# A gated attention and state-space kernel on one core: Toeplitz tiles interleaved by channel, convolution results transposed on PE, exps of 3 and 2 banks

## The chip, the cores and the metric

The kernel runs on one core of a Trainium2 chip. Its time is the device time of one execution in microseconds (us). Besides the timed runs there is one profiled execution; all rows below come from it. PE is the matrix engine, PEld its weight loads, ACT the scalar engine (here it computes the exponentials), DVE the vector engine, POOL the general engine and SP the engine that issues most DMAs. PE writes its results to PSUM, which has eight banks of 128 partitions by 512 fp32 numbers; everything else that the engines read lies in SBUF, and DMAs move data between SBUF and DRAM.

## The reference, cut to what matters

```python
x = A_x                                             # 1 x 2048 x 448, bf16
g = sigmoid((x * gate_w).sum(-1, keepdims=True))
q = (x @ wq) in 16 heads of 28;  k = x @ wk;  v = x @ wv     # one key and value head for all
a = softmax(q k^T / sqrt(28)) v, heads joined, @ wo
P = exp(dt * A * l)                                 # 448 x 256 modes, l = 0..2047, complex
K = Re(sum_n C_n P_nl (dt B_n))                     # 448 x 2048: one filter per channel
b = causal_conv(x, K) per channel + x * Dskip
out = g * a + (1 - g) * b
```

The attention has 16 heads over 2048 x 2048 scores. The state-space part (SSM) builds a filter of 2048 taps for each of the 448 channels from 256 complex modes, and convolves each channel of x with its filter.

## The kernel before, in words

**Order of the work.** The program is a list of operations, each with an engine, a cost in ns and keys that it reads and writes. `Prog.schedule` (L104) plays the list through with these costs: of all operations whose inputs are done it takes the one that can start first, and between equals the one with the lower `pr`. The order that comes out is fixed: each engine gets its operations in that order and waits on semaphores of other engines where a key demands it (`emit`, L190). A DMA is planned at 330 bytes per ns and 2 us to land (L55 to L57). A `lock` lets one user after the other hold a PSUM bank. So when an operation is late on the chip, everything behind it on its engine is late too.

**Attention.** The 1024 tiles (4 blocks of 512 queries, 4 groups of 4 heads, 16 key tiles, 4 heads) are cut into 342 batches of 3. `qk` (L842) computes three tiles of scores into banks 0 to 2 or 3 to 5 in turn (L849), ACT takes the exponential of all three in one instruction (L859), and `pv` (L862) multiplies them by the values into bank 6 (`psB`, L874). The three score matmuls of a batch use different 32-row groups of the array, the value matmuls different 32-column groups. After each of 16 groups `norm` (L817) scales by the gate on DVE (L823), sends the denominators through DRAM to spread them (three DMAs in series), and DVE divides (L832) into `onT`. `qproj` (L590) makes the queries two groups ahead, in bank 7 (`psX`).

**SSM.** The channels are cut into 28 chunks of 16. For each, `tables` (L662) raises the modes to powers on DVE by doubling (18 large instructions; `masters` makes the factors for four chunks), and `kgen` (L711) turns them into filters: 64 matmuls (L724) into `psX` in four operations of 16, one DVE copy (L734), four stores to `KP_scratch` in DRAM. `tload` (L741) reads four channels back as a Toeplitz tile: partition p gets the filter from tap p on, which takes a row that starts 2 bytes later for each partition. A tile is 1 MB, loaded by two DMAs of 64 partitions, four runs of 2 KB a partition; four buffers hold tiles (`NTR`). `conv` (L750) multiplies: for each channel 16 blocks of 64 outputs, weights from `U` (x in blocks, 32 columns, zeros where there is no past), moving operand 64 columns of the Toeplitz tile, 64 matmuls a tile (L763), two tiles in one hold of `psX`. DVE copies the result reversed (L770), four stores bring it to `Y_scratch` in DRAM.

`qproj`, `kgen`, `conv` and the projection share `psX` under the lock "X". Chunk `c` of `kgen` and chunk `c - 2` of `conv` are put into the list together, spread evenly between the attention's batches (L893 to L902).

**Output.** After all that the list has, for each of four groups T of 112 channels and each query block qc, `bt` (L778): load y from `Y_scratch` with channels on partitions, add x times Dskip (L786), multiply by 1 - g (L788) into `xT`; and `outg` (L791): for four token tiles four matmuls with Wo (L804) and one with the identity that adds the SSM part (L807), copy (L813), store. T is the outer loop, so the first groups can run once a quarter of the channels is convolved and attention has given `onT`. `osb` has two buffers, `psX` is one bank.

**Start.** `consts` and `loads` zero and load the weights on POOL's queue, x and the raw parameters on SP's and ACT's; `prep_x`, `prep_params` and `prep_attn` transpose x, make the seeds of the modes (`seedz`, `seedw`) and kT, V and the gate. `uload` (L417) loads U for 112 channels by two DMAs with 224-byte runs, four times in the program.

Of the kernel before, what the change touches and what calls it, by code (L numbers as in the profile page):

```python
# [11 lines left out]
P = 128  # L12
# [36 lines left out]
class Op:  # L49
    __slots__ = ("i", "eng", "fn", "ns", "lat", "deps", "pr", "lock", "unlock", "slot", "ndma",  # L50
                 "count", "vc", "end", "nsucc")


class Prog:
    SEM_NS = 60  # L55
    DMA_NS = 2000
    DMA_BW = 330.0  # L57

    def __init__(self, nc, es):
        self.nc, self.es = nc, es  # L60
        self.ops = []
        self.lastw = {}
        self.readers = {}
        self.slots = {}

    def op(self, eng, fn, ns, rd=(), wr=(), pr=0, lat=60, lock=None, unlock=None):
        o = Op()
        o.i, o.eng, o.fn, o.ns, o.lat, o.pr = len(self.ops), eng, fn, ns, lat, pr
        o.lock, o.unlock, o.slot, o.ndma = lock, unlock, None, 0
        deps = {}  # L70
        for k in rd:
            w = self.lastw.get(k)
            if w is not None:
                deps[w] = 1
# [16 lines left out]
    def dma(self, pairs, nbytes, slot, rd=(), wr=(), pr=0, eng="sp", slow=False):  # L91
# [4 lines left out]
        o = self.op(eng, fn, nbytes, rd, wr, pr)  # L96
# [7 lines left out]
    def schedule(self):  # L104
# [15 lines left out]
        locks = {}  # L120
        dmafree = 0.0
        done = 0
        while done < n:
            best = None
            for e in ENG:
                T = free[e]
                for i in ready[e]:
                    o = ops[i]
                    r = max(rt[i], T)
                    if o.lock is not None:  # L130
                        L = locks.setdefault(o.lock, [None, 0.0, []])
                        if L[0] is not None:
                            continue
                        r = max(r, L[1])
                    key = (r, o.pr, i)
                    if best is None or key < best[0]:
                        best = (key, e, i)
            if best is None:
                for L in locks.values():
                    o = ops[L[0]]  # L140
                    print("holder", o.i, o.eng, o.pr, o.fn, [ (j, ops[j].eng, need[j], getattr(ops[j],'end',None)) for j in succ[o.i]])
                    j = [q for q in range(o.i, n) if getattr(ops[q], 'end', None) is None]
                    print([(q, ops[q].eng, ops[q].pr, ops[q].slot, [d for d in ops[q].deps if getattr(ops[d], 'end', None) is None]) for q in j[:30]])
# [9 lines left out]
            order[e].append(i)  # L153
            if o.lock is not None:
# [5 lines left out]
            if o.slot is not None:  # L160
                free[e] = r + 60.0 * o.ndma
                s = max(r, dmafree)
                dmafree = s + o.ns / self.DMA_BW
# [9 lines left out]
            for j in succ[i]:  # L173
# [102 lines left out]
class Kernel:  # L276
# [25 lines left out]
    def alloc(self):  # L302
# [20 lines left out]
        self.rdenB = sb("rdenB", 2 * 512, F32)  # L323
        self.denT = sb("denT", 2 * 16, F32)
        self.onT = sb("onT", 16 * 512, BF)
        self.grow = sb("grow", S, BF)
        self.omg = sb("omg", S, BF)
        self.yT = sb("yT", 2 * 512, BF)
        self.U = sb("U", 2 * 47 * DT, BF)
# [19 lines left out]
        self.osb = sb("osb", 2 * D, BF)  # L349
# [3 lines left out]
        self.Y = nc.dram_tensor("Y_scratch", (D * S,), BF).ap()  # L353
        self.R = nc.dram_tensor("R_scratch", (16 * 4 * 512,), F32).ap()

    def consts(self):
# [16 lines left out]
        pg.op("pool", lambda e: e.memset(V(self.Wq, 0, NT * 512), 0.0), 900, wr=["Wq"])  # L373
        pg.op("pool", lambda e: e.memset(V(self.Wk, 0, NT * P), 0.0), 300, wr=["Wk"])
        pg.op("pool", lambda e: e.memset(self.Wk.v(96, 32, 3 * P + 28, [[32, 4]]), 1.0), 100, wr=["Wk"])
        pg.op("pool", lambda e: e.memset(self.Wk.v(96, 16, 3 * P + 28, [[32, 4]]), 0.0), 100, wr=["Wk"])
        pg.op("pool", lambda e: e.memset(V(self.Wo, 0, NT * D), 0.0), 900, wr=["Wo"])
        pg.op("pool", lambda e: e.memset(V(self.Wb, 0, P), 0.0), 100, wr=["Wb"])
        pg.op("pool", lambda e: e.memset(self.xT.v(96, 32, 3 * S, [[1, S]]), 1.0), 900, wr=["xT3a", "xT3b"])
        pg.op("pool", lambda e: e.memset(self.vaug.v(0, P, 28, [[32, 16]]), 1.0), 100, wr=["va"])  # L380
        pg.op("pool", lambda e: e.memset(self.vaug.v(0, P, 29, [[32, 16], [1, 3]]), 0.0), 100, wr=["va"])
        for s in range(2):
            pg.op("pool", lambda e, s=s: e.memset(self.U.v(0, 64, s * 47 * DT, [[1, 31 * DT]]), 0.0), 2000, wr=[("U", s)], pr=5)
            pg.op("pool", lambda e, s=s: e.memset(self.U.v(64, 64, s * 47 * DT, [[1, 15 * DT]]), 0.0), 2000, wr=[("U", s)], pr=5)
        pg.op("pool", lambda e: e.memset(V(self.kstg, 0, 128), 0.0), 100, wr=[("kst", 0)], pr=5)

    def loads(self):
# [3 lines left out]
        for hf in range(4):  # L391
            pg.dma([(xst.v(0, P, hf * 4 * D, [[D, 4], [1, D]]), dram(x, hf * 4 * P * D, [[D, P], [P * D, 4], [1, D]]))],
                   4 * P * D * 2, f"x{hf}", wr=[("xst", hf)], eng="sp")
        raw = self.onT
        self.names = ["B_A_re", "B_A_im", "B_B_re", "B_B_im", "B_C_re", "B_C_im"]
        pg.dma([(self.dt32.v(0, P, 0, [[1, D]]), dram(ins["B_log_dt"], 0, [[0, P], [1, D]]))], 120000, "ldt", wr=["dt"], eng="act")
        for k, nm in enumerate(self.names):
            pg.dma([(raw.v(0, DT, k * 1024, [[NM, 4], [1, NM]]), dram(ins[nm], 0, [[NM, DT], [DT * NM, 4], [1, NM]]))],
                   D * NM * 2, f"raw{k}", wr=[("raw", k)], eng="act" if k < 2 else "sp", pr=1)
        w = ins["A_wk"]  # L400
        pg.dma([(self.Wk.v(0, DT, 32 * r, [[P, 4], [1, DH]]), dram(w, 0, [[DH, DT], [DT * DH, 4], [1, DH]]))
                for r in range(4)], 400000, "wk", wr=["Wk"], eng="pool")
# [577 lines left out]
```

## Time and profile before

| | us |
|---|---|
| median of 3 runs | 845.64 (844.11 to 847.72) |
| the profiled execution | 844.77 |
| its span, first to last instruction | 843.0 |
| PE busy in the span | 556.3 |
| DVE busy | 525.7 |
| ACT busy | 495.8 |
| POOL busy | 30.1 |

The span is what the profile shows; some 2 us lie around it. Busy times of PE and PEld overlap. The page also has the waits by releaser, the DMA queues and the DMA issues; a time line gives each instruction's start and length from the start of the span.

### The profile page before, as it was taken

The numbers are of one execution on the slowest core, as the hardware profiler recorded it, in microseconds if no ns is written. First come the engines' busy times: TensorE is split into PE (matmuls) and PEld (weight loads), VectorE is DVE, ScalarE is ACT, GpSimd is POOL, SyncE is SP. The second block draws the span as 40 slices with busy tenths as digits, with TensorE's granted clock in tenths as the row PEclk, the third lists the DMA queues.
The fourth block names the chain that finished last, engine by engine and source line by source line (L and its number), as shares of the span: only waits on it lengthen the run. The fifth ranks groups of instructions, "written<-read, shape, count | busy, mean of one in ns | idle before, by whom it ended". The sixth has DMA issues, their size and how long they took to land.

```text
span 843.0 us, 25548 instructions
## 1 busy us (share of the span) xinstructions
PE 556.3 (66%) x11601; PEld 323.5 (38%) x11616; DVE 525.7 (62%) x1153; ACT 495.8 (59%) x362; POOL 30.1 (4%) x43
## 2 busy tenths in 40 slices
PE   5467667676576757686676657774667756758723
PEld 4122333443343423443344334543435334535323
DVE  4999776676576765685576656884667765501311
ACT  3358667574576756575666656774466764838600
POOL 9400000000000000000000000000000000000000
PEclk9655667666686768686667776886687786958755
DMA  9500885998939989988999699888996899999211
GB/s 188 83 1 1 178 176 115 181 203 173 216 74 215 198 160 221 219 175 160 222 189 203 123 222 225 174 173 176 216 217 139 177 219 224 187 219 192 55 30 28
DMA packets 130762, 137.98 MB, mean 164 GB/s; under 512 B 64286, under 2 KB 71022, under 8 KB 130654
## 3 DMA queue, kind: packets, MB, share of 16 engines
q1 hardware_dynamic: 128974, 134.84, 79.1%
q0 software_dynamic: 608, 0.93, 0.9%
q8 instruction: 91, 1.49, 0.9%
q10 hardware_dynamic: 1072, 0.57, 0.3%
q14 instruction: 17, 0.14, 0.1%
HBM read 130.48 MB, written 5.69 MB: 162 GB/s over the span
## 4 chain that ended last, share of the span: by engine, by line
DMA 33%; PE 28%; DVE 17%; issue 10%; SPq 9%; POOL 2%; ACT 1%; ACTq 0%; POOLq 0%
DMA T<-KP_scratch 9%; DMA denT<-acc 9%; SPq L95 9%; PE psX L763 8%; PE psS L849 7%; DMA R_scratch<-denT 5%; PE psB L874 4%; DMA rdenB<-R_scratch 4%; PE psX L724 4%; PE psX L804 2%; DMA yT<-Y_scratch 2%; DVE tmp L688 2%; DMA out_dram<-osb 2%; DVE tab L693 2%; DVE tab L685 2%
## 5 line engine op out<-in xcount | busy, mean ns | idle before, releaser
L859 ACT ACTIVATE expT<-psS 128x1536 bf16<-128x1536 f32 x342 | 479.7, 1452 | 279.2 <-PE psS L849 267.9
L763 PE MATMUL psX<-T,U 128*32 128x64 bf16 x7168 | 198.4, 239 | 155.6 <-issue 76.1
L763 PEld LDWEIGHTS psX<-T,U 128*32 128x32 bf16 x7168 | 161.8, 155 | 184.1 <-issue 81.0
L849 PE MATMUL psS<-qT,kT 29*128 29x512 bf16 x1024 | 172.8, 497 | 34.7 <-issue 13.6
L874 PE MATMUL psB<-expT,vaug 128*32 128x512 bf16 x1024 | 173.2, 497 | 12.1 <-DVE acc L823 6.8
L724 PE MATMUL psX<-tab 128*32 128x64 bf16 x1792 | 80.8, 301 | 26.7 <-issue 10.8
L770 DVE CAST cst<-psX 128x128 bf16<-128x128 f32 x56 | 16.0, 286 | 120.0 <-PE psX L763 116.3
L874 PEld LDWEIGHTS psB<-expT,vaug 128*32 128x32 bf16 x1024 | 35.2, 97 | 129.0 <-issue 116.5
L685 DVE TENSOR_TENSOR tab<-tab,mbf 128x2048 bf16<-128x2048 bf16 (+4 forms) x140 | 78.6, 565 | 0.4
L688 DVE TENSOR_TENSOR tmp<-tab,mbf 128x128 bf16<-128x128 bf16 (+4 forms) x140 | 78.5, 563 | 0.0
L693 DVE TENSOR_TENSOR tab<-tab,tmp 128x128 bf16<-128x128 bf16 (+4 forms) x140 | 77.8, 563 | 0.4
L724 PEld LDWEIGHTS psX<-tab 128*32 128x32 bf16 x1792 | 60.9, 144 | 35.6 <-issue 14.1
L849 PEld LDWEIGHTS psS<-qT,kT 29*128 29x128 bf16 x1024 | 34.6, 95 | 73.4 <-issue 35.4
L804 PE MATMUL psX<-Wo,onT 128*128 128x112 bf16 x256 | 28.6, 282 | 33.2 <-DMA out_dram<-osb 19.1
L828 DVE RECIPROCAL denT<-denT 128x16 f32<-128x16 f32 x16 | 4.0, 252 | 62.1 <-DMA denT<-acc 62.1
L804 PEld LDWEIGHTS psX<-Wo,onT 128*128 128x128 bf16 x256 | 23.7, 136 | 37.8 <-DMA out_dram<-osb 21.5
L701 DVE TENSOR_TENSOR tab<-tab,mbf 128x2048 bf16<-128x2048 bf16 x28 | 34.1, 1218 | 0.0
L703 DVE TENSOR_TENSOR tmp<-tab,mbf 128x2048 bf16<-128x2048 bf16 x28 | 34.1, 1217 | 0.0
L708 DVE TENSOR_TENSOR tab<-tab,tmp 128x2048 bf16<-128x2048 bf16 x28 | 34.0, 1215 | 0.0
L832 DVE TENSOR_TENSOR onT<-acc,rdenB 128x512 bf16<-128x512 f32 x16 | 11.1, 692 | 36.0 <-DMA rdenB<-R_scratch 35.9
L813 DVE CAST osb<-psX 128x448 bf16<-128x448 f32 x16 | 9.9, 620 | 34.8 <-PE psX L807 34.7
L657 DVE TENSOR_TENSOR mbf<-mst,sgn 128x256 bf16<-128x256 f32 x70 | 29.1, 416 | 0.0
(95 smaller groups left out, 341.6 us busy)
## 6 DMA issues: line engine op xcount, KB each, us to landing
T<-KP_scratch SPq DMA_DIRECT2D x224, 512.0 KB, 10.7
rdenB<-R_scratch SPq DMA_DIRECT2D x64, 64.0 KB, 4.3
tab<-in_A_x_dram SPq DMA_DIRECT2D x4, 448.0 KB, 10.5
U<-in_A_x_dram SPq DMA_DIRECT2D x4, 448.0 KB, 8.4
KP_scratch<-kstg SPq DMA_DIRECT2D x112, 16.0 KB, 7.6
Y_scratch<-cst SPq DMA_DIRECT2D x112, 16.0 KB, 9.9
yT<-Y_scratch SPq DMA_DIRECT2D x16, 112.0 KB, 8.1
out_dram<-osb SPq DMA_DIRECT2D x16, 112.0 KB, 2.1
```

Of the source, the lines that this page charges most:

```text
L95: return [e.dma_start(o, i, **kw) for o, i in pairs]
L685: pg.op("dve", lambda e, d=dst3, a=src, m=m, w=w: e.tensor_tensor(d, a, mbf.v(0, P, m, [[HC, 4], [0, w], [1, HC]]), ALU.mult), el(n, 1.92) ...
L688: pg.op("dve", lambda e, a=src, m=m, w=w: e.tensor_tensor(tmp.v(0, P, so, [[w * HC, 4], [HC, w], [1, HC]]), a, mbf.v(0, P, m + 128, [[HC, ...
L693: pg.op("dve", lambda e, d=d2, t=t2: e.tensor_tensor(d, d, t, ALU.add), el(n, 1.92), rd=[("tmp", s), ("tab", s, lv + 1)], wr=[("tab", s, l ...
L701: pg.op("dve", lambda e: e.tensor_tensor(dst, src, mbf.v(0, P, m, [[HC, 2], [0, 32], [1, HC]]), ALU.mult), el(n, 1.92), rd=rk + mk, wr=[(" ...
L703: pg.op("dve", lambda e: e.tensor_tensor(tmp.v(0, P, so, [[BLK, 2], [HC, 32], [1, HC]]), src, mbf.v(0, P, m + 64, [[HC, 2], [0, 32], [1, H ...
L724: r = e.matmul(self.psX.v(32 * j, 32, 64 * g, [[1, 64]]), tab.v(0, P, to + (4 + comp) * BLK + o, [[HC, 32]]), tab.v(0, P, to + comp * BLK ...
L763: r = e.matmul(self.psX.v(32 * j, 32, 64 * k, [[1, 64]]), self.U.v(0, P, uo + (15 - mm_) * DT + d, [[DT, 32]]), self.T.v(0, P, s * 4096 + ...
L804: e.matmul(ov, self.onT.v(0, P, (qc * 4 + g) * 512 + 128 * tt, [[1, 128]]), self.Wo.v(0, P, g * D + DT * T, [[1, DT]]), start=(g == 0), st ...
L849: r = e.matmul(self.psS.v(0, P, 1536 * s + 512 * k, [[1, 512]]), kT.v(32 * h, DH + 1, 128 * kt, [[1, 128]]), qT.v(32 * h, DH + 1, 512 * qs ...
L859: pg.op("act", lambda e: e.activation(expT.v(0, P, 1536 * es, [[1, n]]), self.psS.v(0, P, 1536 * s, [[1, n]]), AF.Exp, scale=SQ), 185 + n ...
L874: r = e.matmul(self.psB.v(32 * h, 32, 0, [[1, 512]]), vaug.v(0, P, 32 * kt, [[1, 32]]), expT.v(0, P, 1536 * es + 512 * k, [[1, 512]]), sta ...
```

## The change

- **Toeplitz tiles.** The filters of four channels are interleaved in DRAM, so a partition of a tile is one run of 8 KB (four channels side by side, 4096 numbers) and the rows of neighbouring partitions start 8 bytes apart. The moving operand of a convolution matmul then takes every fourth number. `kgen` writes runs of 512 bytes for that. `NTR` is 3.
- **U** is loaded once for all channels by 48 DMAs with 896-byte runs, newest block first; the weights of a convolution matmul have `32 - m_` columns instead of 32 with zeros.
- **Convolution results.** A whole chunk (four tiles) accumulates in bank 5 under a lock "C" of its own. DVE copies it times 1 - g (`omq`). `ytr` transposes it by 8 matmuls into `psX`, and DVE adds it to `O`, which holds the whole output with tokens on partitions (16 x 448 numbers, bf16). `Y_scratch`, `bt`'s loads and `osb` go.
- **Exps.** Batches have 3 and 2 tiles in turn (410 in all): banks 0 to 2, and 3 and 4.
- **Projection.** `outp` computes one token tile with all 448 channels and adds it to `O`; three query blocks are put into the list as soon as the next one has begun, the last at the end in banks 0 to 3. 16 stores of 112 KB follow, each after all additions to `O`.
- **Start.** POOL's memsets and the weight loads move to DVE and SP, with Wq and Wk loaded dense and spread by DVE; scratch memory of `prep_params` moves to U and O.
- **Planner.** A DMA is planned by number and size of its packets; PE and DVE operations with `pr` of 2 and more are planned 500 and 300 ns after their inputs; additions to `O` may come in any order (`comm`).

```diff
     SEM_NS = 60
-    DMA_NS = 2000
-    DMA_BW = 330.0
+    DMA_NS = 2200
+    SLACK = {"pe": 500.0, "dve": 300.0}
...
+        nd, size = desc
+        o = self.op(eng, fn, nd * (30.0 + 0.03 * size if size < 1500 else 105.0 + 0.022 * size) / 16.0 * 1.1, rd, wr, pr)
...
+                    if x.pr >= 2:
+                        t += self.SLACK.get(x.eng, 0.0)
...
-        self.NTR = 4
+        self.NTR = 3
         self.T = sb("T", self.NTR * 4096, BF)
...
+    def uload(self):
+        for k in range(3):
+            lst = []
+            for p in range(16):
+                if k == 0:
+                    hb, pos, blk = 0, p, 15 - p
+                else:
+                    hb, pos, blk = 1, p + 16 * (k - 1), 31 - p - 16 * (k - 1)
+                lst.append((self.U.v(64 * hb, 64, pos * D, [[1, D]]), dram(x, 64 * blk * D, [[D, 64], [1, D]])))
+            pg.dma(lst, (1024, 896), f"u{k}", rd=["sw", "Uz"], wr=["U"], pr=2)
...
+        pg.op("dve", lambda e: e.tensor_copy(self.omq.v(0, P, 0, [[1, 64]]), t.v(0, P, o, [[1, 64]])), el(64),
+              rd=[("b", 6)], wr=["omq"], pr=0.8)
...
+        pg.dma([(dram(self.KP, (4 * c + g) * 4 * KPW, [[256, 32], [1, 256]]),
+                 self.kstg.v(32 * g, 32, ks * 256, [[1, 256]])) for g in range(4)],
+               (128, 512), f"kw{ks}", rd=[("kst", ks)], wr=[("KP", c)], pr=0)
...
-        pg.dma([(self.T.v(64 * h, 64, s * 4096, [[1024, 4], [1, 1024]]),
-                 dram(self.KP, d0 * KPW + 1024 * h, [[1, 64], [KPW, 4], [1, 1024]])) for h in range(2)],
-               128 * 8192, f"T{s}", rd=[("KP", c), "pad"], wr=[("T", s)], pr=1)
...
+        pg.dma([(self.T.v(64 * h, 64, s * 4096, [[1, 4096]]),
+                 dram(self.KP, 4 * gi * KPW + 4096 * h, [[4, 64], [1, 4096]])) for h in range(2)],
+               (128, 8192), f"T{s}", rd=[("KP", c), "pad"], wr=[("T", s)], pr=1)
+
+    def ytr(self, c):
+        pg = self.pg
+        cs = c % 2
+        X = ("yx", c)
+
+        def mm(e):
+            for k in range(4):
+                for par in range(2):
+                    r = e.matmul(self.psX.v(64 * par, 64, 64 * k, [[1, 64]]),
+                                 self.cst.v(0, P, cs * 256 + 64 * k, [[1, 64]]),
+                                 self.ident.v(0, P, 1 - par, [[32, 4], [2, 16]]),
+                                 start=True, stop=True, tile_position=(0, 64 * par), skip_group_check=True)
+            return r
+        pg.op("pe", mm, 400, rd=[("cst", cs), "id"], wr=[X], pr=3.5, lock="X")
+        ov = self.O.v(0, P, 15 * D + 16 * c, [[-D, 16], [1, 16]])
+        pg.op("dve", lambda e: e.tensor_tensor(ov, ov, self.psX.v(0, P, 0, [[1, 16], [16, 16]]), ALU.add),
+              el(256), rd=[X], comm="O", pr=2, unlock="X")
+
+    def conv(self, c):
+        pg = self.pg
+        X = ("cx", c)
+        cs = c % 2
+        ps, po = self.bank(5)
+        for k in range(4):
...
+            self.tload(gi)
             for m in range(0, 16, 2):
                 def mm(e, k=k, m=m, s=s, gi=gi):
+                    for m_ in (m, m + 1):
                         for j in range(4):
-                            r = e.matmul(self.psX.v(32 * j, 32, 64 * k, [[1, 64]]),
-                                         self.U.v(0, P, uo + (15 - mm_) * DT + d, [[DT, 32]]),
-                                         self.T.v(0, P, s * 4096 + j * 1024 + 960 - 64 * mm_, [[1, 64]]),
+                            r = e.matmul(ps.v(32 * j, 32 - m_, po + 64 * k, [[1, 64]]),
+                                         self.U.v(0, P, m_ * D + 4 * gi + j, [[D, 32 - m_]]),
+                                         self.T.v(0, P, s * 4096 + (960 - 64 * m_) * 4 + j, [[4, 64]]),
+                                         start=(m_ == 0), stop=(m_ == 15), tile_position=(0, 32 * j), skip_group_check=True)
                     return r
+                first = k == 0 and m == 0
+                pg.op("pe", mm, 130, rd=[("T", s), "U"], wr=[X, ("cst", cs)] + ([("b", 5)] if c == 0 else []) if first else [X], pr=4,
+                      lock="C" if first else None)
+        pg.op("dve", lambda e: e.tensor_tensor(self.cst.v(0, P, cs * 256, [[64, 4], [1, 64]]),
+                                               ps.v(0, P, po + 63, [[64, 4], [-1, 64]]),
+                                               self.omq.v(0, P, 0, [[0, 4], [1, 64]]), ALU.mult),
+              el(256), rd=[X, "omq"], wr=[("cst", cs)], pr=2, unlock="C")
+        self.ytr(c)
...
+        def mm(e):
+            for g in range(4):
+                e.matmul(t.v(0, P, o, [[1, D]]), self.onT.v(0, P, so + g * 512 + 128 * tt, [[1, 128]]),
+                         self.Wo.v(0, P, g * D, [[1, D]]), start=(g == 0), stop=False,
+                         tile_position=(0, 0), skip_group_check=True)
+            for T in range(NT):
+                r = e.matmul(t.v(0, P, o + DT * T, [[1, DT]]),
+                             self.xT.v(0, DT, T * S + 512 * qc + 128 * tt, [[1, 128]]),
+                             self.ident.v(0, DT, 0, [[1, DT]]), start=False, stop=(T == 3), tile_position=(0, 0), skip_group_check=True)
             return r
+        pg.op("pe", mm, 1700, rd=["Wo"] + [("xq", T, qc) for T in range(4)] + [("on", (qc % 2) * 4 + g) for g in range(4)],
+              wr=[X] + kb, pr=2, lock=lock)
+        ov = self.O.v(0, P, D * (4 * qc + tt), [[1, D]])
+        pg.op("dve", lambda e: e.tensor_tensor(ov, ov, t.v(0, P, o, [[1, D]]), ALU.add), el(D), rd=[X] + kb, comm="O", pr=2, unlock=lock)
...
+    def store(self, i):
+        self.pg.dma([(dram(self.out, i * P * D, [[D, P], [1, D]]), self.O.v(0, P, D * i, [[1, D]]))],
+                    (128, 896), f"out{i}", rd=["O"], pr=1)
...
+        bt, i = [], 0
+        while i < len(tiles):
+            n = 2 if len(bt) % 2 else 3
+            bt.append(tiles[i:i + n])
+            i += n
...
+                if i and i % 4 == 0:
+                    for tt in range(4):
+                        self.outp(i // 4 - 1, tt, 7)
...
+        for tt in range(4):
+            self.outp(3, tt, tt)
+        for i in range(16):
+            self.store(i)
```

## Rows read from the trace of the kernel before

**Rows 1.** The page, part 1: busy us (share of the span) and instructions of each engine
```profile
PE 556.3 (66%) x11601; PEld 323.5 (38%) x11616; DVE 525.7 (62%) x1153; ACT 495.8 (59%) x362; POOL 30.1 (4%) x43
```

**Rows 2.** Stretches of the loop and the tail: busy us per engine, clock, DMA share, GB/s
```profile
46.80:798.40 751.60, 518.66 (x11289) 296.37 (x11303) 485.12 (x1091) 480.29 (x343) 0.00 (x0) 0.72 0.86 174
798.40:843.00 44.60, 15.83 (x161) 13.78 (x161) 6.63 (x11) 0.00 (x0) 0.00 (x0) 0.55 0.12 27
```

**Rows 3.** The page, parts 3 and 6: DMA queues; issues with us to landing
```profile
q1 hardware_dynamic: 128974, 134.84, 79.1%
q8 instruction: 91, 1.49, 0.9%
...
T<-KP_scratch SPq DMA_DIRECT2D x224, 512.0 KB, 10.7
...
out_dram<-osb SPq DMA_DIRECT2D x16, 112.0 KB, 2.1
```

**Rows 4.** Waits over the span: engine, line, waited for: total us, times, longest
```profile
ACT expT L859 <- PE psS L849: 267.9, 152, 10.5
...
PE psX L763 <- issue: 76.1, 29, 5.6
...
PE psX L763 <- DMA T<-KP_scratch: 31.3, 17, 5.1
...
PE psX L763 <- DVE kstg L734: 21.5, 6, 6.6
...
PE psX L763 <- DVE cst L770: 20.4, 6, 10.5
```

**Rows 5.** Time line of PE: start, length, what [idle before, what ended it]
```profile
357.39 0.42 PE L724 MATMUL psX<-tab 128*32 128x64 bf16 x6 [3.72 <-issue]
```

**Rows 6.** Two stretches of 20 us, columns as in rows 2
```profile
240.00:260.00 20.00, 15.06 (x375) 9.70 (x377) 19.73 (x42) 16.34 (x12) 0.00 (x0) 0.93 0.51 111
...
760.00:780.00 20.00, 17.52 (x474) 11.24 (x476) 2.63 (x6) 17.03 (x13) 0.00 (x0) 0.86 0.94 188
```

**Rows 7.** DMA queue q1 from 112 to 130 us, then from 804.5 to 808.5
```profile
q1 hardware_dynamic: 2014, 3.80, 102.9%
...
q1 hardware_dynamic: 193, 0.26, 21.8%
```

**Rows 8.** Groups of instructions: count, busy us, mean ns, idle before, by what
```profile
L859 ACT ACTIVATE expT<-psS 128x1536 bf16<-128x1536 f32 x342 | 479.7, 1452 | 279.2 <-PE psS L849 267.9 <-PE psB L874 8.4
L763 PE MATMUL psX<-T,U 128*32 128x64 bf16 x7168 | 198.4, 239 | 155.6 <-issue 76.1 <-DMA T<-KP_scratch 31.3 <-DVE kstg L734 21.5
...
L724 PE MATMUL psX<-tab 128*32 128x64 bf16 x1792 | 80.8, 301 | 26.7 <-issue 10.8 <-DVE cst L770 8.5 <-DVE tab L708 5.8
```

**Rows 9.** Time line of PE at two places, score and value groups
```profile
65.45 0.61 PE L849 MATMUL psS<-qT,kT 29*128 29x512 bf16 x3 [0.19 <-ACT expT L859]
65.99 0.61 PE L874 MATMUL psB<-expT,vaug 128*32 128x512 bf16 x3
...
782.06 0.39 PE L849 MATMUL psS<-qT,kT 29*128 29x512 bf16 x3
782.38 0.40 PE L874 MATMUL psB<-expT,vaug 128*32 128x512 bf16 x3
```

**Rows 10.** Time line near and in the tail: a store's issue, onT, a projection's copy
```profile
785.98 0.43 SPq L95 DMA_DIRECT2D out_dram<-osb  x1
...
808.21 0.69 DVE L832 TENSOR_TENSOR onT<-acc,rdenB 128x512 bf16<-128x512 f32 x1 [4.79 <-DMA rdenB<-R_scratch]
...
825.53 0.62 DVE L813 CAST osb<-psX 128x448 bf16<-128x448 f32 x1 [4.23 <-PE psX L807]
```

**Rows 11.** Time line of DVE in the start
```profile
19.17 4.71 DVE L504 TENSOR_SCALAR T<-T 128x896 f32<-128x896 f32 x1
...
27.01 0.61 DVE L505 TENSOR_SCALAR T<-T 128x896 f32<-128x896 f32 x1
```

**Rows 12.** Line L763: ns min/median/max, first and last start us
```profile
L763 PE MATMUL psX<-T,U x7168: 189/245/276, 94.2 to 780.1; 128*32 128x64 bf16 x200
```

More of the change, by code (lines that the diff above doesn't have):

```diff
@@ L69, in op @@
         o.lock, o.unlock, o.slot, o.ndma = lock, unlock, None, 0
+        o.comm = comm
         deps = {}
+        if comm is not None:
+            deps[self.lastw[comm]] = 1
+            self.commops.setdefault(comm, []).append(o.i)
         for k in rd:
+            for c in self.commops.get(k, ()):
+                deps[c] = 1
             w = self.lastw.get(k)
@@ L153, in schedule @@
             order[e].append(i)
+            if o.comm is not None:
+                if o.comm in comm:
+                    o.deps[comm[o.comm]] = 1
+                comm[o.comm] = i
             if o.lock is not None:
@@ L397, in loads @@
[L397 to L402, printed above, removed]
-        pg.dma([(self.Wv.v(0, DT, 0, [[32, 4], [1, DH]]), dram(ins["A_wv"], 0, [[DH, DT], [DT * DH, 4], [1, DH]]))],
-               25000, "wv", wr=["Wv"], eng="pool")
@@ L588, in prep_attn @@
                   rd=[("g", qc)], wr=[("g", qc)], pr=0.7)
+        tq = self.kstg.v(0, 32, 256, [[1, 64]])
+        pg.dma([(tq, self.omg.v(0, 1, 0, [[64, 32], [1, 64]]))], (32, 128), "omq",
+               rd=[("g", qc) for qc in range(4)], wr=[("kst", 1)], pr=1)
+        t, o = self.bank(6)
+        pg.op("pe", lambda e: e.matmul(t.v(0, P, o, [[1, 64]]), self.anti.v(0, 32, 0, [[1, P]]), tq,
+                                       start=True, stop=True, tile_position=(0, 0)), 200,
+              rd=["anti", ("kst", 1)], wr=[("b", 6)], pr=0.8)
+        pg.op("dve", lambda e: e.tensor_copy(self.omq.v(0, P, 0, [[1, 64]]), t.v(0, P, o, [[1, 64]])), el(64),
+              rd=[("b", 6)], wr=["omq"], pr=0.8)
     def qproj(self, qc, g):
@@ L767, in mm @@
-                    return r
-                pg.op("pe", mm, 160, rd=[("T", s), ("U", us)], wr=[X, ("cst", c % 2)] if (k == 0 and m == 0) else [X], pr=4, lock="X" if (k == 0 and m == 0) else None)
-        cs = c % 2
-        pg.op("dve", lambda e: e.tensor_copy(self.cst.v(0, P, cs * 256 + 128 * u, [[64, 2], [1, 64]]),
-                                             self.psX.v(0, P, 63, [[64, 2], [-1, 64]])),
-              el(128), rd=[X], wr=[("cst", cs)], pr=2, unlock="X")
-        if u == 1:
-            pg.dma([(dram(self.Y, (16 * c + j) * S, [[64, 32], [4 * S, 4], [1, 64]]),
-                     self.cst.v(32 * j, 32, cs * 256, [[64, 4], [1, 64]])) for j in range(4)],
-                   65536 * 2, f"yw{cs}", rd=[("cst", cs)], wr=[("Y", c)], pr=0)
@@ L779, in bt, with bx @@
+        self.ytr(c)
+    def bx(self, T, qc):
         pg = self.pg
[L780 to L782 removed]
         xv = self.xT.v(0, DT, T * S + 512 * qc, [[1, 512]])
[L784 to L787 removed]
@@ L897, in chunk_step @@
             if 0 <= cc < NCH:
-                if cc % 7 == 0 and cc // 7 + 1 < NT:
-                    self.uload(cc // 7 + 1)
-                for k in range(2):
-                    self.tload(4 * cc + 2 * k)
-                    self.tload(4 * cc + 2 * k + 1)
-                    self.conv(cc, k)
+                self.conv(cc)
         first = 0
@@ L918, in main @@
                 qk(b + 2)
-            t = 3 * b
-            i = t // 64
-            if t % 64 < 3 and i + 2 < 16:
-                self.qproj((i + 2) // 4, (i + 2) % 4)
+            qc, g, kt, h = bt[b][0]
+            i = qc * 4 + g
+            if i >= ndone:
+                ndone = i + 1
+                if i + 2 < 16:
+                    j = i + 2
+                    self.qproj(j // 4, j % 4)
+                    if j % 4 == 3:
+                        for T in range(NT):
+                            self.bx(T, j // 4)
+                if i and i % 4 == 0:
+                    for tt in range(4):
+                        self.outp(i // 4 - 1, tt, 7)
         while c < NCH + LAG:
```

227 lines of the change are left out of this document (99 added, 128 removed).

## The prediction

> **What bounds the kernel now.** I read the table of busy times first, then stretches of the span, the waits, the DMA queues, and last the time lines of single places.
>
> No engine is full: PE is busy 66%, DVE 62%, ACT 59% [rows 1]. The span has three parts: a start of 46.8 us until the first exp, a loop of 751.6 us that holds the 342 exps, and a tail of 44.6 us with ACT empty [rows 2]. In the loop ACT works 480 us, DVE 485 and PE 519, but the DMA engines 86% of the time, and what they move is nearly all Toeplitz loads (224 of 512 KB) [rows 2, 3]. So no engine is the loop's bound; they wait for each other, and for what is to be found.
>
> ACT's idle time is 268 us behind the score matmuls [rows 4]: PE is late. PE itself idles 233 us of the loop (751.6 less 518.7). Its waits [rows 4] are of three kinds: "issue" (76.1 us before convolution matmuls, 28 more in three smaller rows, 104), Toeplitz loads (31), and psX held until DVE has copied it (21.5 + 20.4, 8.5 in a smaller row, 50). "Issue" is no semaphore here: a set of 64 kernel-generation matmuls, issued 16 to an operation, breaks off after 58, inside an operation, and goes on 3.7 us later with the last 6 [rows 5]. The instruction queue moved 91 packets of 16 KB for a PE that ran 11,601 matmuls and 11,616 weight loads [rows 1, 3], one packet for 255 instructions. I read these stalls as PE out of instructions while the fetch stands among the Toeplitz packets. Where such stalls are rare the loop is far better: 12 and 13 exps in 20 us with 375 and 474 matmuls, one of these stretches at a DMA share of 0.51 [rows 6]. The mean of the loop is 9.1.
>
> **The change, part by part.** The sums go by the profiled run: span 843.0, run 844.77, so 1.8 us lie around the span; the median of the runs is 845.64, 0.9 above it.
>
> *Toeplitz loads in 8 KB runs.* 57,344 packets of 2 KB become 14,336 of 8 KB; the bytes stay. In 18 us of nearly nothing else the queue moves 3.80 MB and is busy 102.9% of 16 engines, 296 us, or up to 160 ns a packet of 2 KB [rows 7]. The 128 packets of 2 KB for rdenB, on empty engines, take at most 109 ns (21.8% of 16 x 4 us) [rows 7]. For 8 KB the ends are 109 ns (all cost is per packet) and 667 ns (half a 16 KB instruction packet: 0.9% of 16 x 843 us over 91 [rows 3]). I take 436 ns, four times the packet on empty engines: Toeplitz work falls from 57,344 x 160 / 16 = 573 us to 391, the DMA share of the loop from 0.86 to about 0.6, which is near the stretch of 0.51 in rows 6. With that most of the fetch and load stalls go. NTR goes from 4 to 3: two tiles of lead, at 641 / 112 = 5.7 us each, are 11.4 us against 10.7 to landing today [rows 3]; this cover holds only if loads land sooner. Where it fails a convolution group waits on PE, behind it in PE's order the next score matmul, and for that ACT.
>
> [...]
>
> *A second bank for the SSM.* The convolution gets bank 5 for itself; kernel generation keeps psX with qproj, the new transposes and the projection. The 50 us of psX waits go almost whole; what is late next is the copy of kernel generation when a projection holds psX.
>
> *Exps of 3 and 2 banks.* 410 batches instead of 342. On ACT 1536 columns take 1452 ns [rows 8]; 1024 take between two thirds of that (968, no loss) and all of it (+99 us); the fixed part is small, so I take 1020: 205 x 1452 + 205 x 1020 = 507 us against 497, +10, covered by 271 us of idle ACT in the loop. On PE the three score matmuls of a batch lie in different rows of the array and run side by side (three make one entry of 0.39 or 0.61 us in rows 9), so a batch of two costs what one of three does. A score and a value group take together 0.65 us at best (782.06 to 782.38, doubled) and 1.08 in the slow stretch (65.45 to 65.99, doubled) [rows 9]. 68 more batches are 44 to 73 us of PE; I take 48, near the good stretches, and charge it whole, since PE is the late engine.
>
> *Convolution operands.* 7,168 matmuls stay. The moving operand steps 8 bytes instead of 2, the weights shrink from 32 to 17..32 columns. The nearest row with a stepped moving operand is kernel generation, 64 bytes: 80.8 us / 1792 = 45 ns each against 198.4 / 7168 = 28 [rows 8]. Ends: -45 us, if the weights set the pace (23% of 28 ns), and +125 us, if 8 bytes cost what 64 do. I take 0: 8 bytes are nearer to 2.
>
> [...]
>
> *The Y round trip goes, transposes come.* 112 stores and 16 loads leave SP and the DMA queue. PE gets 224 small matmuls: at best 28 ns each as a convolution one, at worst twice kernel generation's 45, 6 to 20 us; I take 10. DVE gets 28 adds, and 28 larger copies for 56 small ones; even at 1 us more a chunk that is 28 us on an engine with 156 free in 641.
>
> *Output projection.* Twelve of 16 groups move into the loop, where about eight stood already: some 1.2 us each, +5 us on PE. In the tail today each group takes 0.62 + 4.23 = 4.85 us, matmuls, copy, store and its landing in series through one bank, seven times [rows 10]. After: 10.5 us from the last exp to onT as now (798.4 to 808.9, [rows 2, 10]), four groups in four banks, 2.1 us each at the tail's clock of 0.55 (the 4.23 less the landing), 8.4; the last add 0.7; 16 stores, which all wait for that add, 0.43 us of SP issue each [rows 10], 6.9; landing 2.1 [rows 3]. Sum 28.6 against 44.6.
>
> *Start.* POOL's memsets and weight loads go to DVE and SP. The DVE instructions that were slow while POOL worked (4.71 us against 0.61 for its sister [rows 11]) shrink, some 6 us; new memsets and copies cost DVE about 6, half of it before DVE has other work. I take -5: 42 us. U now comes by 48 issues on SP after the seeds, some 20 us, with stores of the first kernels behind them; before the first convolution at 94 us [rows 12] there is room. If not, it costs once what it is late.
>
> *The planner.* It ordered PE's queue with 330 bytes per ns, where rows 7 show 211; it now plans by packets and gives late SSM work slack. Ends: nothing, to the 31 + 50 us counted above; I take no more.
>
> *Sum.* The loop at 12 exps in 20 us is 570 us for 342 exps. Plus 48, 10, 5, and 8 for stalls beyond those of the good stretches: 641. 42 + 641 + 29 + 1.8 = 714. Its own range is 655 to 765: below, 13 exps in 20 us (-44) and a part of the weight gain; above, 73 for the batches and a quarter of the old stalls.
>
> **Rivals.**
> *The loads stay as slow.* For: the halves are as before, and no engine limits rows 7. Against: the same size at 109 ns. DMA work is 79.1% of 843 = 667 us [rows 3]; without Y and with fewer small packets about 630. The convolutions stand between 94 and 780 [rows 12], 686 us, so 97% of it. 630 / 0.97 = 649 us from 89 on: last convolution at 738, last exp 18 later as now, tail 29, 1.8: 787 us.
> *The 8-byte step costs PE.* Place: the convolution matmuls; price 17 ns each, 125 us. PE is then the bound: 519 + 61 (the batches at their mean price) + 15 + 125 busy, and the 104 us of fetch stalls, which go with the number of instructions: a loop of 824, 897 in all. It decides from 10 ns a matmul on, where the loop passes 773. For: kernel generation's row. Against: 64 bytes is far from 8.
> *PE gets no relief.* Fetch stalls stay, only the load and psX waits go, the extra batches eat the rest: 752 - 31 - 50 + 48 + 15 = 734, and 807 in all. For: a low DMA share is seen in one good stretch only. Against: the mid-operation breaks of rows 5.
>
> **How the numbers follow.** Forecast 0.57, loads as slow 0.23, 8-byte step 0.09, no relief 0.11, of which I give a third to times at or above today's. What a measurement of this kernel can tell from no change is about 0.5%, 4 us. Faster 0.87, same 0.03, slower 0.10. The range reaches from 650, a little below the forecast's own, to 805, through the first rival; 2 in 10 lie outside.
>
> **What would show it.** Right: DMA share of the loop near 0.6, packets of 8 KB under 450 ns, "issue" on PE under 60 us, no convolution waiting for kstg or cst, convolution matmuls at 28 ns or less, a tail of 29 us. Wrong: a DMA share still at 0.85 (first rival), convolution matmuls above 38 ns (second), "issue" still 100 us at a low share (third), or a start that grows because U or the seeds come late.

## The result and the profile after

The changed kernel takes 819.16 us (median of 4 runs, 816.14 to 823.75) against 845.62 us for the kernel before: a ratio of 0.969, 95% interval 0.964 to 0.974. It is faster, as forecast, but 105 us slower than the forecast and above its range. The profiled execution took 816.14 us, its span 814.4. Some executions of a kernel took over 1.5% longer than its fastest one; a time below is the median of all executions and a ratio leaves those out, so that the two can differ by about 1%.

Parts 1, 3 and 6 of its page: busy times, the load queue, the tile loads with us to landing.

```profile
PE 636.6 (78%) x11649; PEld 307.7 (38%) x11649; DVE 530.4 (65%) x1156; ACT 506.6 (62%) x430; POOL 1.6 (0%) x12
...
q1 hardware_dynamic: 45928, 132.60, 72.5%
...
T<-KP_scratch SPq DMA_DIRECT2D x224, 512.0 KB, 9.0
```

The loop and the tail, columns as in [rows 2]:

```profile
42.60:787.50 744.90, 607.13 (x11397) 289.05 (x11394) 490.57 (x1084) 490.69 (x410) 0.00 (x0) 0.75 0.77 171
787.50:814.40 26.90, 6.57 (x36) 3.27 (x33) 4.12 (x7) 0.00 (x0) 0.00 (x0) 0.63 0.24 79
```

The start is 42.6 us (forecast 42) and the tail 26.9 (forecast 29). The whole miss is in the loop: 744.9 us where 641 were forecast, after 751.6 in [rows 2]. DMA is at 0.77 there, where the prediction had about 0.6.

The waits, as in [rows 4]:

```profile
ACT expT L915 <- PE psS L905: 247.9, 218, 4.7
...
PE psS L820 <- DMA T<-KP_scratch: 70.5, 52, 3.3
...
PE psS L820 <- issue: 16.4, 13, 3.2
...
PE psX L764 <- issue: 6.0, 4, 2.9
PE psS L820 <- DVE cst L828: 5.9, 2, 4.0
```

Two of the three kinds of stall went as said: "issue" is down from 104 to 28 us (three smaller rows have the other 6), the waits for a bank under copy from 50 to some 7. The third more than doubled: convolutions now wait 70.5 us for Toeplitz tiles, 31.3 before.

Groups, as in [rows 8]:

```profile
L915 ACT ACTIVATE expT<-psS 128x1536 bf16<-128x1536 f32 (+1 forms) x410 | 490.7, 1237 | 254.2 <-PE psS L905 247.9 <-PE psB L929 4.3
L929 PE MATMUL psB<-expT,vaug 128*32 128x512 bf16 x1024 | 207.4, 494 | 23.4 <-ACT expT L915 18.5 <-DVE omq L627 4.0 <-issue 0.4
L905 PE MATMUL psS<-qT,kT 29*128 29x512 bf16 x1024 | 198.1, 484 | 4.2 <-issue 3.8 <-ACT expT L915 0.5
L820 PE MATMUL psS<-T,U 128*32 128x64 bf16 (+15 forms) x7168 | 191.1, 257 | 95.3 <-DMA T<-KP_scratch 70.5 <-issue 16.4 <-DVE cst L828 5.9
...
L797 PE MATMUL psX<-ident,cst 128*64 128x64 bf16 x224 | 10.2, 218 | 4.8 <-issue 1.9 <-DVE qT L650 1.7 <-DVE kstg L774 0.8
```

The 50 us from 700, where the queue carries hardly anything but tiles, and the same stretch in the columns of [rows 2]:

```profile
q1 hardware_dynamic: 2235, 10.30, 95.4%
```

```profile
700.00:750.00 50.00, 34.82 (x790) 17.83 (x778) 3.47 (x8) 27.80 (x23) 0.00 (x0) 0.74 0.96 208
```

10.30 MB in 0.954 x 50 us are 216 GB/s, against 211 in [rows 7] (3.80 MB in 18 us). An 8 KB packet costs 16 x 47.7 us / (10.30 MB / 8192) = 607 ns, where 436 was taken (582 ns is the mean over the whole run). Longer runs bought almost nothing.

### The profile page after: what moved, and what is told of

Read it like the earlier page. It is cut to its first block, busy times and chain, and to the rows that moved or that the text cites. A ratio compares the mean times of both kernels' runs of the same rounds, so it can differ in the third digit from the quotient of the medians.

```text
span 814.4 us, 25556 instructions
## 1 busy us (share of the span) xinstructions
PE 636.6 (78%) x11649; PEld 307.7 (38%) x11649; DVE 530.4 (65%) x1156; ACT 506.6 (62%) x430; POOL 1.6 (0%) x12
## 4 chain that ended last, share of the span: by engine, by line
DMA 38%; PE 38%; DVE 9%; SPq 6%; ACT 5%; issue 4%
DMA T<-KP_scratch 30%; PE psS L820 10%; PE psS L905 9%; PE psB L929 9%; SPq L102 6%; PE psX L764 5%; ACT expT L915 5%; DMA denT<-acc 4%; PE psX L640 2%; DMA rdenB<-R_scratch 2%; DMA R_scratch<-denT 1%; DMA KP_scratch<-kstg 1%; PE psX L851 1%; DVE tab L725 1%; DVE acc L874 1%
## 5 line engine op out<-in xcount | busy, mean ns | idle before, releaser
L915 ACT ACTIVATE expT<-psS 128x1536 bf16<-128x1536 f32 (+1 forms) x410 | 490.7, 1237 | 254.2 <-PE psS L905 247.9
L820 PE MATMUL psS<-T,U 128*32 128x64 bf16 (+15 forms) x7168 | 191.1, 257 | 95.3 <-DMA T<-KP_scratch 70.5
L929 PE MATMUL psB<-expT,vaug 128*32 128x512 bf16 x1024 | 207.4, 494 | 23.4 <-ACT expT L915 18.5
L820 PEld LDWEIGHTS psS<-T,U 128*32 128x32 bf16 (+15 forms) x7168 | 155.5, 182 | 174.3 <-issue 76.6
L905 PE MATMUL psS<-qT,kT 29*128 29x512 bf16 x1024 | 198.1, 484 | 4.2 <-issue 3.8
L929 PEld LDWEIGHTS psB<-expT,vaug 128*32 128x32 bf16 x1024 | 53.0, 116 | 71.3 <-ACT expT L915 53.9
L764 PE MATMUL psX<-tab 128*32 128x64 bf16 x1792 | 65.5, 293 | 8.3 <-issue 6.0
L764 PEld LDWEIGHTS psX<-tab 128*32 128x32 bf16 x1792 | 47.8, 140 | 26.6 <-issue 20.3
L828 DVE TENSOR_TENSOR cst<-psS,omq 128x256 bf16<-128x256 f32 x28 | 11.7, 420 | 63.7 <-PE psS L820 63.7
L879 DVE RECIPROCAL denT<-denT 128x16 f32<-128x16 f32 x16 | 4.0, 253 | 54.8 <-DMA denT<-acc 54.6
L774 DVE CAST kstg<-psX 128x256 bf16<-128x256 f32 x28 | 11.7, 419 | 22.7 <-PE psX L764 22.5
```

Source lines behind the costliest of these rows:

```text
L764: r = e.matmul(self.psX.v(32 * g, 32, 64 * jj, [[1, 64]]), tab.v(0, P, to + (4 + comp) * BLK + o, [[HC, 32]]), tab.v(0, P, to + comp * BLK ...
L820: r = e.matmul(ps.v(32 * j, 32 - m_, po + 64 * k, [[1, 64]]), self.U.v(0, P, m_ * D + 4 * gi + j, [[D, 32 - m_]]), self.T.v(0, P, s * 4096 ...
L905: r = e.matmul(self.psS.v(0, P, 1536 * s + 512 * k, [[1, 512]]), kT.v(32 * h, DH + 1, 128 * kt, [[1, 128]]), qT.v(32 * h, DH + 1, 512 * qs ...
L915: pg.op("act", lambda e: e.activation(expT.v(0, P, 1536 * es, [[1, n]]), self.psS.v(0, P, 1536 * s, [[1, n]]), AF.Exp, scale=SQ), 172 + n ...
L929: r = e.matmul(self.psB.v(32 * h, 32, 0, [[1, 512]]), vaug.v(0, P, 32 * kt, [[1, 32]]), expT.v(0, P, 1536 * es + 512 * k, [[1, 512]]), sta ...
```

## The experiments

Two theories were open: the loads' rate is set by where their rows land (each issue writes one half of the partitions), or by the run length and what else the queue carries. Each experiment was timed beside the kernel before on the same chip; ratios are to that.

**e1: a tile by one issue to all 128 partitions.** The halves are interleaved, taps 0 to 63 on even and 64 to 127 on odd partitions; U has its rows in the same order. Bytes, run length, buffers and matmuls stay.

```diff
-        pg.dma([(self.T.v(64 * h, 64, s * 4096, [[1, 4096]]),
-                 dram(self.KP, 4 * gi * KPW + 4096 * h, [[4, 64], [1, 4096]])) for h in range(2)],
+        pg.dma([(self.T.v(0, P, s * 4096, [[1, 4096]]),
+                 dram(self.KP, 4 * gi * KPW, [[4, 64], [4096, 2], [1, 4096]]))],
```

> Each Toeplitz tile is loaded by one DMA over all 128 partitions (the two halves of taps on even and odd partitions, U in the same order) instead of two DMAs of 64 partitions; 8 KB runs and everything else as in the changed kernel. Theory A (a load that writes 64 partitions is held to about 220 GB/s, whatever its runs): 8 KB packets fall from 582 ns to about 300 to 350, Toeplitz work from 522 us to about 290, waits for Toeplitz loads on PE from 70 us to under 20, time 735 to 775 us. Theory B (the rate is set by the bytes read, from shifted, overlapping rows of DRAM, not by where they are written): packets stay at 560 to 600 ns, time within 5 us of 819.

705.04 us (695.79 to 718.56), ratio 0.828 (0.824 to 0.832), better than any theory had it. The profiled execution is the one of 695.79 us. Its queue in 6 us of little but tiles (468 to 474), its waits for tiles and its loop:

```profile
q1 hardware_dynamic: 329, 2.43, 99.9%
```

```profile
PE psS L823 <- DMA T<-KP_scratch: 16.8, 22, 1.8
```

```profile
41.70:667.50 625.80, 556.22 (x11398) 285.62 (x11395) 488.98 (x1084) 487.45 (x410) 0.00 (x0) 0.87 0.59 204
```

2.43 MB in 6 us are 405 GB/s, nearly twice the rate of the halves, and a packet takes 96 us / 297 = 323 ns there (369 ns over the whole run). Against the changed kernel the loop is 119 us shorter: PE's idle time in it fell from 138 to 70 us, and its busy time from 607 to 556 for the same matmuls, at a mean granted clock of 0.87 instead of 0.75.

**e2: the same in the kernel before**, with its 2 KB runs: four issues a tile, one for each channel, each to 128 partitions.

```diff
-        pg.dma([(self.T.v(64 * h, 64, s * 4096, [[1024, 4], [1, 1024]]),
-                 dram(self.KP, d0 * KPW + 1024 * h, [[1, 64], [KPW, 4], [1, 1024]])) for h in range(2)],
+        pg.dma([(self.T.v(0, P, s * 4096 + 1024 * j, [[1, 1024]]),
+                 dram(self.KP, (d0 + j) * KPW, [[1, 64], [1024, 2], [1, 1024]])) for j in range(4)],
```

> The kernel before, with 2 KB runs, but each Toeplitz DMA over all 128 partitions (one per channel, so four issues a tile instead of two). Theory A: 2 KB packets fall from 156 ns to 82 to 110, PE's fetch stalls and load waits shrink, time 775 to 815 us although the runs are short. Theory B: packets stay near 156 ns and the time near 845, a little above for 224 more issues on SP. If 2 KB packets fall less than 8 KB packets do in the run beside it, run length counts as well.

735.02 us, ratio 0.8723 (0.8691 to 0.8756), 40 us below what was expected. Queue and PE waits:

```profile
q1 hardware_dynamic: 132558, 134.85, 62.5%
```

```profile
PE psX L765 <- DMA T<-KP_scratch: 30.0, 18, 5.3
PE psX L765 <- DVE kstg L736: 26.3, 11, 5.7
...
PE psX L726 <- DVE cst L772: 22.5, 10, 5.3
...
PE psX L765 <- issue: 8.6, 9, 4.0
```

A packet of 2 KB takes 103 ns on average in this trace, against 156 in the one before. So placing alone does far more than the run length (211 GB/s in [rows 7] with 2 KB runs, 216 in the changed kernel with 8 KB). "Issue" almost goes here (9.6 us in all), with four buffers and 2 KB runs: these stalls of [rows 4] do hang on a slow load queue, as the prediction read them. That PE lacks instructions in them is not shown by any run. The waits for psX stay, as they should.

**e10: even and odd partitions, but two issues of 64 again** (the edit against e1).

```diff
-        pg.dma([(self.T.v(0, P, s * 4096, [[1, 4096]]),
-                 dram(self.KP, 4 * gi * KPW, [[4, 64], [4096, 2], [1, 4096]]))],
+        pg.dma([(self.T.two(h, s * 4096, [[1, 4096]]),
+                 dram(self.KP, 4 * gi * KPW + 4096 * h, [[4, 64], [1, 4096]])) for h in range(2)],
```

> The even/odd layout of the 705 us kernel, but each Toeplitz tile loaded by two issues of 64 partitions again: one to the even partitions, one to the odd ones. Theory A (what counts is how far over the partitions the rows reach that are written at one time; the number of issues and rows does not): 705 us within 12, a share of the load queue of the span near 56%. Rival B (an issue of 64 rows is slow wherever its rows lie): 800 to 825 us, share above 70%.

705.78 us, ratio 0.834 (0.828 to 0.839), close to e1 (the intervals overlap). Its queue over the span (the profiled execution took 716.17 us), then from 480 to 486 us:

```profile
q1 hardware_dynamic: 45928, 132.60, 53.9%
```

```profile
q1 hardware_dynamic: 316, 2.03, 81.9%
```

2.03 MB in 0.819 x 6 us are 413 GB/s, the rate of e1. The number of issues and of rows in one is not it. This kernel and the changed one load the same rows by the same two issues of 64; only the partitions on which they land differ (every second one against one half).

**e9: one issue, halves left in their places.** This was to tell the same apart, without moving U.

```diff
+        pg.dma([(self.T.v(0, P, s * 4096, [[1, 4096]]),
+                 dram(self.KP, 4 * gi * KPW, [[4096, 2], [4, 64], [1, 4096]]))],
```

> The changed kernel with one edit: each Toeplitz tile is loaded by ONE DMA to 128 partitions whose halves stay where they are (taps 0 to 63 on partitions 0 to 63, 64 to 127 on the upper ones); U and the convolutions are untouched. Theory A (what a single DMA spans sets its rate; two issues to 64 partitions each are slow even when both are under way): as with the even/odd layout, 705 us within 10, packets of 8 KB near 370 ns, PE's waits for Toeplitz tiles 15 to 25 us. Rival B (it is the order of the partitions: only neighbouring rows for different halves spread the load): 790 to 820 us, packets near 580 ns.

2445.51 us, ratio 2.90: neither theory. In a stretch of its loop, columns as in [rows 2]:

```profile
1000.00:1100.00 100.00, 29.07 (x528) 13.53 (x525) 18.62 (x41) 21.07 (x17) 0.00 (x0) 0.57 0.14 57
```

PE waits for tiles in 1610 of 2444 us, and the DMA engines are busy 0.14 at 57 GB/s: as much as two full ones of the 16 (0.125) and a little. The source's outermost dimension is 2 here, where it was 64; whether that is the cause no run tests by itself. The run says nothing on the question it was made for.

**e5: no tile loads after the third.**

```diff
+            if gi < self.NTR:
+                self.tload(gi)
```

> The changed kernel without 109 of its 112 Toeplitz tile loads (the convolution uses what lies in the three buffers). If the loads pace the loop: 710 to 750 us, which is then all that any faster load can give, and the waits of PE that are left are not for DMAs. If they do not: above 800 us.

657.75 us (2 runs), far below what was expected: what free loads would give, with an order that is also planned without them. PE is then busy 87% of the span, DVE 80%, and of the "issue" before PE's matmuls 2.4 us are left.

**e7: the planner told the price of a tile.** The changed kernel's planner takes a tile at 2.51 us of the queue (128 packets at 285 ns, over 16, times 1.1); the chip takes 4.66 for packets at 582 ns, a mean over all of them.

```diff
-               (128, 8192), f"T{s}", rd=[("KP", c), "pad"], wr=[("T", s)], pr=1)
+               (238, 8192), f"T{s}", rd=[("KP", c), "pad"], wr=[("T", s)], pr=1)
```

> The changed kernel with one number of its planner changed: a Toeplitz tile is priced at 4.66 us of the queue (14,336 packets at 582 ns over 16 engines and 112 tiles) instead of 2.51, so that PE's order is made for the loads as they are. Theory A (the load queue sets the end, whatever the order): 819 us within 5. Rival B (the wrong price puts convolutions ahead of the scores that could run meanwhile, and the order costs it): 785 to 805 us.

762.75 us, ratio 0.907 (0.901 to 0.912) where it was 0.969: some 53 us from one number, with loads as slow as ever, more than rival B had. The queue from 640 to 730 us, its loop and the rest, and the waits for tiles in each of the two:

```profile
q1 hardware_dynamic: 3652, 19.76, 100.0%
```

```profile
42.70:651.50 608.80, 539.17 (x10070) 261.64 (x10067) 483.85 (x1072) 484.69 (x410) 0.00 (x0) 0.85 0.79 177
651.50:758.10 106.60, 35.79 (x1362) 29.57 (x1360) 9.10 (x19) 0.00 (x0) 0.00 (x0) 0.55 0.92 208
```

```profile
PE psS L820 <- DMA T<-KP_scratch: 1.5, 3, 0.8
...
PE psS L820 <- DMA T<-KP_scratch: 53.4, 18, 4.4
```

19.76 MB in 90 us of a full queue: 220 GB/s. The exps end at 651.5 instead of 787.5, and the last tiles trail. With the true price the planner puts scores where it had put convolutions whose tiles were not there; PE keeps its order, so such a convolution holds up ACT too. The waits for tiles fell only to 54.8 us, but 53.4 of them now stand after the last exp, where no score is behind them; in the changed kernel all 70.5 stand in the loop.

**e13: the same in the kernel before** (`DMA_BW` 330 to 206; here one number prices all DMAs).

> The kernel before with one number changed: its planner reckons the loads at 206 GB/s, about as measured, instead of 330. Theory A (in both kernels PE's order was made for loads that are faster than the real ones, and it costs a few per cent): 795 to 825 us, PE waits for tiles below 20 us. Rival B (only the changed kernel, whose planner takes a tile at half its price, suffers; the kernel before is held by fetch stalls and psX): 838 to 850 us.

793.91 us, ratio 0.940 (0.935 to 0.945), a little better than theory A, though its 20 us of waits did not come: they doubled, from 31.3. The waits over the span, then the loop and the rest:

```profile
PE psX L763 <- DMA T<-KP_scratch: 60.9, 26, 4.4
PE psX L763 <- issue: 49.6, 28, 4.6
```

```profile
48.90:619.00 570.10, 443.60 (x9103) 244.86 (x9118) 460.49 (x1030) 469.26 (x342) 0.00 (x0) 0.83 0.85 171
619.00:786.00 167.00, 64.61 (x2299) 56.26 (x2291) 22.14 (x48) 0.00 (x0) 0.00 (x0) 0.51 0.93 208
```

The first of these lines is the same when only 619.0 to 786.0 is asked for: all 60.9 us of waits for tiles come after the last exp. The other waits fell: "issue" from 104 to 81 us, psX under copy from 50 to some 12. So the total of a wait does not say what it costs: what matters is what stands behind it.

**e4: the kernel before with three buffers** (`NTR` 3, memory as before).

> The kernel before with its Toeplitz tiles rotating through 3 buffers instead of 4 (same memory set aside). Theory A (the first rival's 787 us came out at 819 because three buffers keep the load queue less busy): 860 to 880 us, PE waits for Toeplitz tiles 60 to 80 us instead of 31. Rival B (the buffer count is not it; the shorter wait chain or something else of the change is): 843 to 852 us.

842.91 us, ratio 1.000 (0.997 to 1.002): rival B's time, with theory A's waits for tiles. The waits changed places:

```profile
PE psX L763 <- DMA T<-KP_scratch: 82.4, 33, 7.0
PE psX L763 <- issue: 43.7, 24, 4.0
```

With smaller rows "issue" is 56 us instead of 104, and tiles 82 instead of 31: together 138 and 136. With fewer tiles under way "issue" costs less and the tiles come later. So part of the fall of "issue" in the changed kernel can be the third buffer's, and is no gain.

**e3: batches of 3, convolutions back in psX**, loads as in the change (`n = 3`, `self.bank(7)`, lock "X").

> The changed kernel with 342 batches of 3 tiles as before, and the convolution back in psX under the lock X, one hold per chunk. If the second bank is worth more than the 68 batches cost: slower than 819, 830 to 850, with some 50 us of PE waits for the copies out of psX. If loads pace the loop and both are hidden: within 5 us of 819. If the extra batches' 50 to 60 us of PE are on the path: 775 to 805.

843.29 us, ratio 1.001 (0.999 to 1.003), in the first range, though the waits for copies out of psX are some 22 us and not 50, and those for tiles grew instead. With slow loads the second bank and the smaller batches are worth some 27 us by the ratios, and the rest of the change, with its planner as it is, nothing that can be measured.

```profile
PE psX L820 <- DMA T<-KP_scratch: 125.8, 53, 4.7
```

**e6: the same on top of e1.**

> The whole-tile loads (705 us) with 342 batches of 3 and the convolutions back in psX under one hold a chunk. Theory A (with fast loads PE is the bound, and 68 batches at 48 to 60 us of PE are more than the second bank is worth): 665 to 690 us, PE busy near 525 us. Rival B (the psX waits come back, 50 us as in the kernel before, and eat it): 700 to 725 us.

705.64 us, ratio 0.838 (0.834 to 0.841), against 0.828 for e1: rival B's time, but not its reason, since the psX waits come to some 17 us. PE saves 42 us (542.4 busy, 583.9 in e1) and gives them back: waits for tiles are 48.4 us where e1 has 16.8, and the convolutions run on to 696 when the last exp began at 621.5 (each line's times, then its first and last start):

```profile
L823 PE MATMUL psX<-T,U x7168: 217/252/317, 87.2 to 696.0; 128*21 128x64 bf16 x16, 128*19 128x64 bf16 x14, 128*32 128x64 bf16 x13, 128*23 128x64 bf16 x13
```

```profile
L918 ACT ACTIVATE expT<-psS x342: 598/1451/1495, 42.8 to 621.5; 128x1536 bf16<-128x1536 f32 x171
```

**e14: e1 without the planner's slack** (500 and 300 ns to 0).

> The whole-tile loads (705 us) with the planner's slack for late SSM work (500 ns on PE, 300 ns on DVE) set to zero. Theory A (the slack keeps PE and DVE from stopping behind work that comes a little late; without it the loop has 13 to 20 exps' worth of such stops): 715 to 740 us. Rival B (the slack changes nothing that can be measured): 700 to 710 us.

717.52 us, ratio 0.852 (0.847 to 0.857) against 0.828: some 20 us slower than e1 by the ratios, and in theory A's range. Waits for tiles are 35 us instead of 17.

```profile
PE psS L823 <- DMA T<-KP_scratch: 35.2, 28, 3.5
```

**e11: e1 with the tile's price raised to its own 2.96 us.**

> The whole-tile loads (705 us) with the planner's price for a Toeplitz tile raised from 2.51 to 2.96 us (8 KB packets at 369 ns, over 16 engines). Theory A (a price below the loads' real one costs PE stalls behind late tiles, as in the changed kernel, in proportion): PE's 17 us of waits for tiles go down, 690 to 700 us. Rival B (with loads this fast the order hardly hangs on them): 700 to 710 us.

691.45 us (685.67 to 695.86, 6 runs), ratio 0.820 (0.816 to 0.824): the best time with all its loads, 128 us below the changed kernel. The step from e1 is small (0.828, 0.824 to 0.832; the intervals touch), some 7 us by the ratios, and the waits for tiles did not fall:

```profile
PE psS L823 <- DMA T<-KP_scratch: 19.6, 15, 4.7
```

## Why the prediction was wrong

| us (ratio to before) | planner as it was | loads priced as measured |
|---|---|---|
| before, halves | 845.6 (1) | 793.9 (0.940) |
| changed, halves | 819.2 (0.969) | 762.8 (0.907) |
| changed, even/odd | 705.0 (0.828) | 691.5 (0.820) |

**The step that failed: "I take 436 ns, four times the packet on empty engines."** It measured 607 ns (700 to 750 us of the changed kernel), 582 over the whole run: 522 us of Toeplitz work instead of 391. The 109 ns of [rows 7] came from rdenB, four issues that together went to all quarters of the partitions, on engines 21.8% busy; a row from another placing and an emptier queue was carried over to loads that go to halves. Of these two differences the placing counts: e2's 2 KB packets on all partitions take 103 ns under load. The prediction's other row, 211 GB/s for halves, was the one of the same placing, and it held at 8 KB: 216 and 220 GB/s. From there followed the tile waits and the loop: in e1, which changes only where the rows land, the DMA share of the loop becomes 0.59 and the ratio 0.828, where 714 us were 0.844. That e1 lands so near the forecast is partly luck: its packets cost 323 to 369 ns and not 436, so it is no test of the rest of the sum.

The DMA share of "about 0.6" rests on a slip, too: 0.86 of 751.6 us less the 182 us of Toeplitz work to be saved leaves 464 us, which are 0.62 of the old loop but 0.72 of the forecast loop of 641 us. With its own term the prediction should have expected a queue far busier than the 0.51 of [rows 6].

The first rival's premise, that halves stay as slow, should have had more than 0.23: the one row of the same placing spoke for it. The runs show 216 to 220 GB/s for halves, 405 for rows over all partitions (e1), and 413 with two issues of 64 (e10), which ties this to the partitions and not to the size of an issue. Why halves are slower is not shown.

**The second step: the planner, "I take no more" than the waits already counted.** It plans a tile at 3.18 us before (1 MB at 330 bytes per ns) and at 2.51 after, where the chip takes about 5 and 4.66. By the ratios the true price is worth some 53 us in the changed kernel and 51 in the one before, and e7 alone brings the time into the predicted range with the loads as slow as they are. With fast loads the price is worth only some 7 us (e1, e11), so the two steps cannot be added. The prediction had seen 330 against 211 GB/s, and missed that the new price is further off than the old one; even its own 436 ns make 128 x 436 / 16 = 3.49 us a tile.

**The first rival** had the right cause (the loads stayed at 216 to 220 GB/s) and 787 us instead of 819. Its working assumes a queue that is hardly ever empty, 649 us of convolutions. In e7 they run from 97.9 to 746.8, which is 649 too, but by luck: the queue's work there is 77.4% of 758, 587 us and not 630, which is 0.90 of the convolutions' time and not 0.97. In the changed kernel, planned for faster loads, they run from 92.5 to 758.5. With the order mended (e7) the rival is undercut, since the exps then end long before; so the order of the work accounts for the 32 us and more. The third buffer cost the kernel before nothing (e4); it was not tried alone in the changed one.

**"PE gets no relief"** lies nearest (807), but for a reason that did not happen: "issue" went from 104 to 28 us. **The 8-byte step**, together with the narrower weights, costs nothing: 191.1 us for 7,168 matmuls, 198.4 in [rows 8]. Single ones take 257 ns instead of 239, but they run side by side. The two were not tried apart, so neither the 45 us that narrower weights might have given nor the price of the step is shown alone; that it is 0 was the author's estimate.

**What held.** Start 42.6 (42), tail 26.9 (29), transposes 10.2 us (10), exps 490.7 against 479.7 (+11; +10 forecast): one of 1536 columns takes 1453 ns, one of 1024 takes 1023, where 1020 was taken. The 68 batches cost PE 60 us, inside the 44 to 73: the value and score groups of the page before were

```profile
L849 PE MATMUL psS<-qT,kT 29*128 29x512 bf16 x1024 | 172.8, 497 | 34.7 <-issue 13.6
L874 PE MATMUL psB<-expT,vaug 128*32 128x512 bf16 x1024 | 173.2, 497 | 12.1 <-DVE acc L823 6.8
```

346.0 us, against 405.5 after. The 48 that the forecast charged was 12 too little. The waits for psX went as said, 50 to some 7.

**Where the expected gain went.** The loop lost 95 us of PE's idle time (233 to 138) and got 88 us more of busy time (519 to 607), at a clock of 0.75. Only some 32 us of that are longer groups (the sums of all PE groups over the span are 718 and 751 us: 60 for the batches, 10 for the transposes, less for generation, convolution and projection); for the rest, groups overlap less. With fast loads the same work takes 556 busy at 0.87. Whether PE's idling behind tiles lowers that clock was not separated here. What stays open too is how much of the 76 us less of "issue" is the third buffer (48 in e4) and how much the rest of the change.

## What to carry to other kernels

Take a transfer's price from rows that land on the same partitions under a like load, not from rows of the same size (8 KB packets took 582 ns in halves and 369 in e1). Where an order is planned ahead, compare each planned duration with the trace before anything else: one number of the planner moved both kernels by some 50 us, twice what the whole edit did. And judge a wait by what is queued behind it: e13 doubled its waits for tiles, all of them after the last exp, and gained 6%.

## What the hardware showed that was not expected

- Two issues of 64 rows each give 216 to 220 GB/s when one writes the lower half and the other the upper half of the partitions, and 405 GB/s (e1, one issue) or 413 (e10, two issues) when the halves alternate on even and odd partitions; the ratios are 0.828 and 0.834.
- One issue of 128 rows whose source has an outermost dimension of 2 keeps 0.14 of the DMA engines busy, 57 GB/s (e9, 1000 to 1100 us).
- In the 64-partition loads runs of 8 KB are hardly better than runs of 2 KB (216 to 220 and 211 GB/s).
